# Attention, low-rank mixing and a two-layer MLP on one core: seven products instead of eight in one more part, with the input sums made earlier and the decoding placed by a table

## The chip, the cores and the metric

The kernel runs on one core of a Trainium2 chip. A core has five engines that each work through their own instructions in order and wait for one another by semaphores: TensorE (PE in the rows; PEld is its loading of weights, which overlaps the matmuls), VectorE (DVE), ScalarE (ACT), GpSimd (POOL) and SyncE (SP), whose queue issues the DMAs. The metric is the device time of one execution in microseconds (us), here the median of three runs.

## The reference

```python
# attention: 4 batches, 12 heads, 448 positions, head_dim 64
scores = scale * np.matmul(q, k.transpose(0, 1, 3, 2))
scores = np.where(causal_mask, -1000000000.0, scores)
attn = softmax(scores)
x = (attn @ v).transpose(0, 2, 1, 3).reshape(B, S, 768)
# low-rank mixing over positions: U (448 x 32), V (32 x 448)
h = x.transpose(0, 2, 1) @ U @ V
u = x + h.transpose(0, 2, 1)
# MLP: w_ch1 (768 x 3072), w_ch2 (3072 x 768)
ch = np.maximum(u @ w_ch1, 0.0) @ w_ch2
return u + ch
```

The weights arrive as 64-bit floats and are turned into 32-bit floats on the chip.

## The kernel before

**Stages.** Attention runs first, pair of heads by pair of heads. Then comes the MLP in two groups: `mlp()` for batches 0 and 1, `strassen()` for batches 2 and 3. The end of attention and of the mixing for the last batch (the *drain*) is woven into the first part of `mlp()`.

**The first group.** `mlp()` goes through the hidden units in six parts p = 0 to 5. A part has a first layer (four weight blocks n = 8p to 8p+3, 128x768 each) and a second layer (four more). Each number is split into a high and a low half, and a product is three matmuls (high-high, high-low, low-high). In a *plain* part the first layer takes both batches and both halves of the input rows by themselves: 4 blocks x 2 batches x 18 = 144 matmuls of 448 columns. In a part of `QUADS` (`range(3, FS - 1)`: p = 3 and 4) `quad()` uses Strassen's scheme with seven products instead of eight: two sets of 7 products x 9 = 126 matmuls. The second layer has 144 in both kinds. `quad()` needs sums of weight blocks (`sums13`, `sums24` in `quad_steps`, on VectorE, into `b_sums`), their split halves (`high` on ScalarE, `lows` on VectorE, for the four operands A1, S23, S1, A2 of a set) and sums of the inputs (tiles `T`, made once by `t_rounds`); its results pass through `r` and `r2`, where VectorE adds the products that share an output.

**Steps.** `mlp()` yields after each matmul, and nine of them are a *step* i, a tick of some 1.83 us. At each step the main loop emits what `schedule()` filed under it in `timed`, then the pending ReLUs, a share of the attention that is left (`DRAIN` = 32: it is spread over 32 steps), a round of `t_rounds`, a round of `u_rounds` (input sums for the second group) and, near the end, the first preparations for the second group. So the order on each engine is the order of emission.

**Decoding.** A block is loaded by `load_w` (SP queue), turned into bits by `w_bits` (two ScalarE and three VectorE instructions), added up by `w_sum` (GpSimd, tile `wa`, and a store to `kept` on the SP queue), and split by `w_high` (ScalarE) and `w_low` (VectorE, then a store to `halves`). `schedule()` gives `w_bits` fixed distances to the part's begin (`BITS`, or a pace of 13 or 16 steps in four blocks), and `w_sum` comes two steps later. `home(n)` names one of four places for `wa`.

**Input sums.** `t_rounds(kc)`, kc = 0 to 2, loads two kept pieces of the inputs from `plain_x`, makes two sums, splits them, makes two more and splits those: six rounds. Their tiles lie in the pools `b_top` and `b_late`, which open when the drain is over; a round is emitted every third step from then on (steps 37 to 88). The pool `b_early` opens when the last `values` of attention frees the heads' room.

## Time and profile before

| | before |
|---|---|
| median of 3 runs | 847.87 us (847.28 to 847.97) |
| the profiled execution | 846.55 us, its span 844.8 us |
| PE busy | 837.7 us (99%), 4708 instructions |
| PEld busy | 745.4 us (88%) |
| DVE busy | 690.9 us (82%) |
| ACT busy | 452.4 us (54%) |
| POOL busy | 234.5 us (28%) |
| DMA | 166.65 MB, mean 197 GB/s |

The busy time of an engine is a sum over stages that differ; the first group of the MLP lies between about 172 and 531 us of the span. A wait that the profile shows on one engine matters where TensorE waits in the end.

### The profile page before, as it was taken

Reading aid. Unit: us, or ns where it says so; the run is one execution under the profiler, and the core shown is the slowest. Engines: PE = TensorE matmul, PEld = TensorE weight load, DVE = VectorE, ACT = ScalarE, POOL = GpSimd, SP = SyncE. Lnnn points to the kernel's source line nnn. Section 1 sums busy time; section 2 is a strip of 40 time slices with the busy share of each in tenths; the row PEclk is TensorE's granted clock in tenths of the full one; section 3 lists DMA queues with packets and bytes.
Section 4 is the critical chain, followed back from the end, with each engine's and each line's share of the span. In section 5 each row is a group of like instructions: output and inputs, shape, how many; then the busy total and the mean of one; then the engine's idle time right before and its main releaser. Section 6 shows DMA issues by size and latency. Waiting matters only on the chain.

```text
span 844.8 us, 13959 instructions
## 1 busy us (share of the span) xinstructions
PE 837.7 (99%) x4708; PEld 745.4 (88%) x4708; DVE 690.9 (82%) x1436; ACT 452.4 (54%) x978; POOL 234.5 (28%) x305
## 2 busy tenths in 40 slices
PE   8999999999999999999999999999999999999998
PEld 6778777788999998998999999999999999999997
DVE  7988988965767888997988887698887887886795
ACT  7999999854325454546463553361533515335420
POOL 4765777732111223222312342010000001001100
PEclk9999999999999999999999999999999999999999
DMA  6554253475669777768764569944554544655334
GB/s 208 182 180 147 89 166 121 132 276 207 231 233 318 277 265 238 295 247 314 245 225 188 195 237 331 321 144 145 155 174 125 156 145 138 191 167 163 91 88 143
DMA packets 75816, 166.65 MB, mean 197 GB/s; under 512 B 7009, under 2 KB 49633, under 8 KB 75745
## 3 DMA queue, kind: packets, MB, share of 16 engines
q1 hardware_dynamic: 75744, 165.77, 58.3%
q8 instruction: 37, 0.61, 0.3%
q14 instruction: 35, 0.28, 0.1%
HBM read 104.79 MB, written 55.44 MB: 190 GB/s over the span
## 4 chain that ended last, share of the span: by engine, by line
PE 95%; DVE 3%; issue 1%; ACT 1%; POOL 0%; DVEq 0%; ACTq 0%; POOLq 0%
PE sa L1022 21%; PE of L726 21%; PE hf L666 13%; PE se L1022 10%; PE s L268 6%; PE t L322 5%; PE pv L338 5%; PE sb L1022 5%; PE ba L691 3%; PE y L396 1%; PE be L691 1%; PE bb L691 1%; DVE wsp L473 1%; PE xt L379 1%; DVE p L283 1%
## 5 line engine op out<-in xcount | busy, mean ns | idle before, releaser
L201 POOL TENSOR_TENSOR wa<-wld 128x768 int32<-128x768 int32 (+1 forms) x49 | 77.6, 1583 | 257.1 <-DVE wld L189 141.8
L726 PE MATMUL of<-g,wsp 128*128 128x448 f32 x630 | 132.7, 366 | 0.4 <-DVE wsp L473 0.3
L726 PEld LDWEIGHTS of<-g,wsp 128*128 128x128 f32 x630 | 117.9, 188 | 10.6 <-DVE wsp L473 1.5
L311 POOL TENSOR_SCALAR p<-p,r 112x112 f32<-112x112 f32 (+3 forms) x188 | 94.3, 522 | 56.9 <-DVE r L305 33.9
L818 POOL TENSOR_TENSOR wsp<-wld,wsp 128x256 fp32r<-128x256 f32 (+1 forms) x30 | 30.2, 1010 | 279.9 <-ACT wsp L968 159.5
L297 ACT ACTIVATE p<-p,m 112x112 f32<-112x112 f32 (+1 forms) x192 | 99.8, 527 | 8.6 <-DVE m L283 8.6
L1022 PE MATMUL sa<-h,wsp 128*128 128x448 f32 (+1 forms) x438 | 98.1, 364 | 0.0
L1022 PE MATMUL sa<-uch,wsp 128*128 128x448 f32 x288 | 88.8, 369 | 0.0
L1022 PEld LDWEIGHTS sa<-h,wsp 128*128 128x128 f32 x438 | 81.6, 188 | 6.9
L283 DVE CUSTOM_DVE_ANT_0 p<-s,mask 112x112 f32<-112x112 f32 x192 | 75.1, 445 | 12.4 <-PE s L268 9.5
L935 ACT CAST wsp<-sw 128x256 fp32r<-128x256 f32 (+3 forms) x60 | 34.1, 577 | 79.4 <-PE sa L1022 36.3
L666 PE MATMUL hf<-wsp 128*128 128x448 f32 x288 | 62.1, 368 | 0.0
L666 PE MATMUL hf<-u,wsp 128*128 128x448 f32 x288 | 61.4, 366 | 0.0
L484 ACT CAST wsp<-wa 128x768 fp32r<-128x768 f32 x34 | 28.3, 833 | 61.2 <-POOL wa L201 49.3
L1022 PEld LDWEIGHTS sa<-uch,wsp 128*128 128x128 f32 x288 | 54.1, 188 | 5.9 <-ACT r L1043 1.0
L818 DVE TENSOR_TENSOR xb<-sa,xb 128x448 f32<-128x448 f32 (+1 forms) x73 | 44.7, 615 | 17.1 <-PE sa L1022 16.8
L322 PE MATMUL t<-ident,p 112*112 112x112 f32 x480 | 56.7, 262 | 1.1 <-DVE p L311 0.7
L666 PEld LDWEIGHTS hf<-u,wsp 128*128 128x128 f32 x288 | 53.9, 188 | 4.3
L666 PEld LDWEIGHTS hf<-wsp 128*128 128x128 f32 x288 | 53.5, 188 | 4.3 <-DVE wsp L473 0.2
L737 DVE TENSOR_TENSOR xa<-of,xa 128x448 f32<-128x448 f32 x72 | 42.2, 617 | 18.4 <-PE of L726 18.4
L183 ACT ACTIVATE wa<-wld 128x768 f32<-128x768 f32 (+1 forms) x49 | 44.2, 902 | 23.3 <-DMA wld<-in_w_dram 11.7
L268 PE MATMUL s<-qk 64*112 64x224 f32 (+3 forms) x384 | 53.8, 415 | 0.8 <-DMA qk<-in_qk_dram 0.8
(150 smaller groups left out, 1785.5 us busy)
## 6 DMA issues: line engine op xcount, KB each, us to landing
wld<-in_w_dram SPq DMA_DIRECT2D x48, 768.0 KB, 6.0
kept<-wa SPq DMA_DIRECT2D x48, 384.0 KB, 3.2
halves<-wsp SPq DMA_DIRECT2D x23, 768.0 KB, 4.4
wsp<-halves SPq DMA_DIRECT2D x36, 384.0 KB, 4.1
wsp<-halves SPq DMA_DIRECT2D x54, 256.0 KB, 3.2
qk<-in_qk_dram SPq DMA_DIRECT2D x23, 448.0 KB, 4.8
wld<-kept SPq DMA_DIRECT2D x24, 384.0 KB, 4.5
wld<-kept SPq DMA_DIRECT2D x72, 128.0 KB, 2.8
```

The costliest lines, as they stand in the source:

```text
L183: nc.scalar.activation(f(a), f(hi), AF.Abs)
L201: nc.gpsimd.tensor_tensor(a.bitcast(I32), t[:, :n, 1].bitcast(I32), t[:, :n, 0].bitcast(I32), op=ALU.add)
L268: nc.tensor.matmul(o, t[r, q0 : q0 + CP], t[r, S // 2 : S // 2 + n], start=True, stop=True, skip_group_check=True,)
L283: nc.vector.tensor_tensor_reduce(out=st["p", b, h][:, POFF[i] : POFF[i] + n], in0=st.pop(("o", b, h, i)), in1=mask[:, S - n :], scale=-(D* ...
L297: nc.scalar.activation(pi, pi, AF.Exp, bias=m[:, i : i + 1], scale=-1.0, accum_out=l[:, i : i + 1])
L311: e.tensor_scalar(pi, pi, r[:, i : i + 1], 1.0, op0=ALU.mult, op1=ALU.mult)
L322: nc.tensor.transpose(o[:, n : n + CP], src, ident[:CP, :CP])
L338: nc.tensor.matmul(o[j * D : (j + 1) * D, kt * CP : S], v[:, kt, j, :], pt[:, n0 : n0 + S - kt * CP], start=j not in begun, stop=not left[ ...
L666: nc.tensor.matmul(o, w[:, l, cs], m, start=(kc + i == 0), stop=(kc + i == NC + 1))
L726: nc.tensor.matmul(o[k, b], w[:, l, cs], g[:, v], start=(half + m + i == 0), stop=(half + m + i == 4), skip_group_check=True,)
L818: (nc.vector if e == "V" else nc.gpsimd).tensor_tensor(o, a, b, op=op)
L1022: nc.tensor.matmul(st[bank, q][:, part], a, b[:, part], start=(n in FIRST and ms[0] == 0 and k == 0), stop=(n in LAST and end and k == len ...
```

## The change

`QUADS` begins at 2 instead of 3, so part 2 takes seven products too. To have the input sums by then, `t_rounds` runs in steps 16 to 53 (`T_AT`), and its tiles lie in a pool `b_in` that opens with the heads' room. Its rounds for one kc now follow one another. The step of each `w_bits` stands in a table (`BIT_AT`, 48 numbers), the distance to `w_sum` in another (`GAPS`), and that of each round of `u_rounds` in a third (`U_AT`, steps 141 to 183; before: every second step from 143 to 177). `DRAIN` is 34. The moves of x to `xr` in the drain are issued from the ScalarE queue. The first group has 186 steps instead of 188. Instructions that only check the order at build time (`owner`, `summed`) put nothing on the chip.

```diff
-DRAIN = 32
+DRAIN = 34
...
+T_LOADS = (15, 18, 35)
+T_AT = (16, 22, 23, 24, 25, 26, 27, 31, 32, 35, 38, 39, 41, 43, 46, 49, 51, 53)
...
-QUADS = range(3, FS - 1)
+QUADS = range(2, FS - 1)
...
-        nc.sync.dma_start(out=f(t), in_=st["x", b, c])
+        e = nc.scalar if "draining" in st else nc.sync
+        e.dma_start(out=f(t), in_=st["x", b, c])
...
-        if p in QUADS or p + 1 == QUADS[0]:
+        if 12 <= n <= 8 * QUADS[-1] + 7:
             return (2, 3, 0, 1)[j % 4]
-        return (j + (p == 0)) % 2
+        return (j + (p < QUADS[0])) % 2
...
-                bits = [(n0 + j, c + y) for j, y in enumerate(BITS)]
...
-                pace = 13 if p + 1 == QUADS[0] else 16
-                bits = [(n0 + j, c + pace * j // 4 - 7) for j in range(8)]
...
-            for n, y in bits:
-                sums[n] = y + 2
+            for n in range(n0, n0 + 8):
+                y = BIT_AT[n]
+                sums[n] = y + GAPS[n]
                 if n > 1:
                     at(y, w_bits, n)
-                    at(y + 2, w_sum, n)
+                    at(sums[n], w_sum, n)
...
         def loads():
...
+            if kc < 2:
+                tags = (("T24h1", "T24l1"), ("T13h2", "T13l2"))[kc]
+                x.extend(st["b_in"].tile([P, 2, S], F32, tag=tag, name="x") for tag in tags)
+            else:
+                x.extend((st["r"][:, :2], st["r2"]))
+            for y, c in zip(x, (kc, kc + NC // 2)):
+                for b in range(2):
+                    nc.sync.dma_start(out=y[:, b], in_=plain_x[c][:, b * S : (b + 1) * S])
...
-        return loads, [sums13, high("13"), lows("13")], [sums24, high("24"), lows("24")]
+        return loads, [sums13, high("13"), lows("13"), sums24, high("24"), lows("24")]
...
                 if step == values and a == pairs[-1]:
                     heads.close()
-                    b_pool(b_early, "b_early")
+                    b_pool(b_in, "b_in", "left")
+                    for kc in range(NC // 2):
+                        load, more = t_rounds(kc)
+                        at(T_LOADS[kc], load)
+                        rounds += more
...
-            if rounds and i >= t_begin and i % 3 == 1:
+            if i in T_AT:
                 rounds.pop(0)()
...
-            if us and US(i):
+            if i in U_AT:
                 for step in us.pop(0):
                     step()
```

**PE, the first layer of part 2.** Before, these rows stand between the second layers of parts 1 and 2 (`hf`: plain results; `wsp`: split weights; `u`, `g`: inputs of the two layers).

```order
L726 MATMUL of<-g,wsp 128x448 x144
L666 MATMUL hf<-wsp 128x448 x18
L666 MATMUL hf<-u,wsp 128x448 x18
L666 MATMUL hf<-wsp 128x448 x18
L666 MATMUL hf<-u,wsp 128x448 x18
L666 MATMUL hf<-wsp 128x448 x18
L666 MATMUL hf<-u,wsp 128x448 x18
L666 MATMUL hf<-wsp 128x448 x18
L666 MATMUL hf<-u,wsp 128x448 x18
L726 MATMUL of<-g,wsp 128x448 x144
```

After, the same place begins so (`ba`, `bb`, `be`: the shared outputs of the seven products; `wh`: two further places for split weights).

```order
L746 MATMUL of<-g,wsp 128x448 x144
L711 MATMUL ba<-wsp,wh 128x448 x9
L711 MATMUL bb<-wsp,wh 128x448 x9
L711 MATMUL ba<-T,wh 128x448 x9
L711 MATMUL be<-T,wh 128x448 x9
L711 MATMUL ba<-T,wsp 128x448 x9
L711 MATMUL ba<-wsp,wh 128x448 x9
L711 MATMUL bb<-wsp,wh 128x448 x9
L711 MATMUL ba<-u,wsp 128x448 x9
L711 MATMUL be<-T,wsp 128x448 x9
L711 MATMUL ba<-T,wh 128x448 x9
L711 MATMUL be<-T,wh 128x448 x9
```

Eight groups of 18 have become fourteen groups of 9, the last two of which stand between pieces of the second layer.

**DVE, steps 15 to 21 of the drain.** Before: a decoding (three rows that end in L189) follows `y`, the low half of the mixing's intermediate, which TensorE waits for at its next `hm`.

```order
L654 SCALAR_TENSOR_TENSOR g<-hf,g 128x448
L419 TENSOR_TENSOR xb<-hm,xb 128x448
L473 TENSOR_TENSOR wsp<-wa,wsp 128x768
L409 TENSOR_TENSOR y<-y 64x256
L185 TENSOR_SCALAR wa<-wa 128x768
L187 TENSOR_SCALAR wa<-wa 128x768
L189 SCALAR_TENSOR_TENSOR wld<-wld,wa 128x768
L388 TENSOR_TENSOR xn_l<-xt,xn_h 112x4x128
L737 TENSOR_TENSOR xa<-of,xa 128x448
```

After:

```order
L674 SCALAR_TENSOR_TENSOR g<-hf,g 128x448
L190 TENSOR_SCALAR wa<-wa 128x768
L192 TENSOR_SCALAR wa<-wa 128x768
L194 SCALAR_TENSOR_TENSOR wld<-wld,wa 128x768
L479 TENSOR_TENSOR wsp<-wa,wsp 128x768
L425 TENSOR_TENSOR xb<-hm,xb 128x448
L840 TENSOR_TENSOR x<-x 128x448 x2
L415 TENSOR_TENSOR y<-y 64x256
L757 TENSOR_TENSOR xa<-of,xa 128x448
L479 TENSOR_TENSOR wsp<-wa,wsp 128x768
```

The first two input sums (L840) now stand ahead of `y`, one step behind the issue of their loads on the SP queue:

```order
L490 DMA kept_102<-wa 128x768
L804 DMA x<-plain_x 128x448 x4
L472 DMA halves_150<-wsp 128x1536
L490 DMA kept_103<-wa 128x768
L804 DMA x<-plain_x 128x448 x4
L178 DMA wld<-in_w_dram 128x1536
```

The loads stand behind the store of the fifth block's sum; before, none stood in the drain.

**DVE, steps 26 to 31.** Before: the decodings of blocks 8 and 9 are one each, with only the outputs' sums (`xa`, `xb`) and one low half between them.

```order
L185 TENSOR_SCALAR wa<-wa 128x768
L187 TENSOR_SCALAR wa<-wa 128x768
L189 SCALAR_TENSOR_TENSOR wld<-wld,wa 128x768
L419 TENSOR_TENSOR xb<-hm,xb 128x448 x2
L737 TENSOR_TENSOR xa<-of,xa 128x448
L419 TENSOR_TENSOR xb<-hm,xb 128x448
L737 TENSOR_TENSOR xa<-of,xa 128x448 x2
L473 TENSOR_TENSOR wsp<-wa,wsp 128x768
```

After:

```order
L479 TENSOR_TENSOR T<-x,T 128x896
L425 TENSOR_TENSOR xb<-hm,xb 128x448
L840 TENSOR_TENSOR x<-x 128x448 x2
L757 TENSOR_TENSOR xa<-of,xa 128x448
L190 TENSOR_SCALAR wa<-wa 128x768
L192 TENSOR_SCALAR wa<-wa 128x768
L194 SCALAR_TENSOR_TENSOR wld<-wld,wa 128x768
L425 TENSOR_TENSOR xb<-hm,xb 128x448
L757 TENSOR_TENSOR xa<-of,xa 128x448 x2
L479 TENSOR_TENSOR wsp<-wa,wsp 128x768
L190 TENSOR_SCALAR wa<-wa 128x768
L192 TENSOR_SCALAR wa<-wa 128x768
```

An input sum's low half (`T`) and two further input sums have come in, and a second decoding follows the first at once.

## Rows read from the trace of the kernel before

**Rows 1.** The page: busy us of each engine, and the granted TensorE clock by slices.

```profile
PE 837.7 (99%) x4708; PEld 745.4 (88%) x4708; DVE 690.9 (82%) x1436; ACT 452.4 (54%) x978; POOL 234.5 (28%) x305
PEclk9999999999999999999999999999999999999999
```

**Rows 2.** Timeline of PE where parts 1 to 5 begin (start us, us).

```profile
244.62 0.57 PE L666 MATMUL hf<-wsp 128*128 128x448 f32 x2
...
302.99 0.97 PE L666 MATMUL hf<-wsp 128*128 128x448 f32 x4
...
362.02 1.99 PE L691 MATMUL ba<-wsp,wh 128*128 128x448 f32 x9
...
417.44 1.98 PE L691 MATMUL ba<-wsp 128*128 128x448 f32 x9
...
472.50 0.97 PE L666 MATMUL hf<-wsp 128*128 128x448 f32 x4
```

**Rows 3.** Waits of PE and of PEld, 160 to 535 us: total, times, longest.

```profile
PE of L726 <- DVE wsp L473: 0.3, 1, 0.3
...
PEld of L726 <- DVE wsp L473: 1.5, 3, 0.7
```

**Rows 4.** Busy us of PE, PEld, DVE, ACT, POOL, clock, DMA: parts 2, 3.

```profile
302.99:362.00 59.01, 58.70 (x289) 53.98 (x288) 53.55 (x74) 29.48 (x40) 17.01 (x10) 1.00 0.76 271
362.00:417.20 55.20, 55.05 (x270) 50.41 (x270) 48.92 (x75) 30.42 (x46) 12.49 (x8) 1.00 0.76 273
```

**Rows 5.** DVE groups of part 3, 362 to 417 us: count, busy us, mean ns.

```profile
L473 DVE TENSOR_TENSOR wsp<-sums,wsp 128x384 fp32r<-128x384 f32 x4 | 4.3, 1077 | 0.0
...
L818 DVE TENSOR_TENSOR sums<-wa 128x384 f32<-128x384 f32 x4 | 2.0, 546 | 0.0
L473 DVE TENSOR_TENSOR wh<-sums,wh 128x768 fp32r<-128x768 f32 x2 | 1.9, 974 | 0.0
L818 DVE TENSOR_TENSOR r<-bb,r 128x448 f32<-128x448 f32 x2 | 1.2, 622 | 1.5 <-ACT wa L183 1.5
```

**Rows 6.** Timeline of the SP queue and of DVE around step 16.

```profile
210.50 0.32 SPq L480 DMA_DIRECT2D kept<-wa  x1
...
212.78 0.47 SPq L370 DMA_DIRECT2D xr<-xb  x1
...
211.38 0.96 DVE L473 TENSOR_TENSOR wsp<-wa,wsp 128x768 fp32r<-128x768 f32 x1 [0.33 <-ACT wsp L484]
...
219.91 0.63 DVE L737 TENSOR_TENSOR xa<-of,xa 128x448 f32<-128x448 f32 x1 [4.09 <-PE of L726]
```

**Rows 7.** DMA issues of the page: KB of one, median us to landing.

```profile
xr<-xa SPq DMA_DIRECT2D x12, 224.0 KB, 2.3
...
r<-plain_x SPq DMA_DIRECT2D x3, 224.0 KB, 5.5
...
sums<-plain_x SPq DMA_DIRECT2D x1, 224.0 KB, 6.8
```

**Rows 8.** Busy us of each engine, steps 20 to 34 (columns as in rows 4).

```profile
219.91:249.05 29.14, 29.14 (x150) 26.99 (x149) 20.97 (x35) 7.89 (x12) 4.40 (x3) 1.00 0.52 183
```

**Rows 9.** DVE groups of part 2, 303 to 362 us: decodings, input sums' low halves.

```profile
L189 DVE SCALAR_TENSOR_TENSOR wld<-wld,wa 128x768 uint32<-128x768 uint32 x10 | 9.6, 960 | 0.4
...
L187 DVE TENSOR_SCALAR wa<-wa 128x768 uint32<-128x768 uint32 x10 | 5.6, 560 | 0.3
...
L473 DVE TENSOR_TENSOR T<-x,T 128x896 fp32r<-128x896 f32 x3 | 3.2, 1083 | 0.0
```

**Rows 10.** Timeline at two input sums, with the GpSimd addition beside the second.

```profile
325.57 0.62 DVE L818 TENSOR_TENSOR x<-x 128x448 f32<-128x448 f32 x1
...
325.87 1.64 POOL L201 TENSOR_TENSOR wa<-wld 128x768 int32<-128x768 int32 x1 [5.20 <-ACT g L650]
326.22 1.77 DVE L818 TENSOR_TENSOR x<-r,x 128x448 f32<-128x448 f32 x1
```

**Rows 11.** Timeline of DVE at step 3 of the drain.

```profile
183.28 0.63 DVE L654 SCALAR_TENSOR_TENSOR g<-hf,g 128x448 fp32r<-128x448 f32 x1 [3.63 <-ACT g L650]
```

**Rows 12.** DVE groups of the first group, 165 to 535 us: second group's input sums.

```profile
L818 DVE TENSOR_TENSOR ucl<-tmp,uch 128x896 fp32r<-128x896 f32 x6 | 8.7, 1450 | 0.0
```

More of the change, by code (lines that the diff above doesn't have):

```diff
@@ L473, in low @@
         (nc.vector if BE[key] == "V" else nc.gpsimd).tensor_tensor(o, a, b, op=ALU.subtract)
+    summed, owner = set(), {}
     def w_bits(n):
+        assert owner.get(home(n)) is None
+        owner[home(n)] = n
         st["wa", n] = decode_bits(st["wr", n], WB, home(n))
@@ L480, in w_sum, with used_up @@
         nc.sync.dma_start(out=kept[n], in_=f(st["wa", n]))
+        summed.add(n)
+    def used_up(n):
+        owner[home(n)] = None
+        return st.pop(("wa", n))
     def w_high(n, i):
+        assert n in summed
         t = st["w", n] = slot(i)
@@ L487, in w_low @@
         t = st["w", n]
-        low(key, t[:, 1], f(st.pop(("wa", n))), f(t[:, 0]))
+        low(key, t[:, 1], f(used_up(n)), f(t[:, 0]))
         keep_split(n, t)
@@ L543, in sums13 @@
         def sums13():
+            assert top in summed and bottom in summed
             s = st["b_sums"]
@@ L551, in sums24 @@
             adder(s[:, 3], a(1), s[:, 0], ALU.subtract)
+            owner[home(top)] = None
         def high(name, i, *parts):
             def step():
+                assert top in summed
                 if name not in g:
@@ L640, in activated @@
             return st["u1", 0][:, 0]
[L641 to L642 removed]
+        if n == 3 and b == 1:
+            pool, tag = (st["b_late"], "g13") if p else (st["b_in"], "T24l2")
+        else:
+            pool, tag = main, f"g{b}{n}"
+        return pool.tile([P, 2, S], F32R, tag=tag, name="g")
     def mlp():
@@ L770, in t_rounds @@
     def t_rounds(kc):
-        if kc:
-            x = st["b_late"].tile([P, 2 * WB], F32, tag=f"slot{kc + 1}", name="x")
-            x = x[:, : 3 * S].rearrange("p (i s) -> p i s", i=3)
-        else:
-            x = st["r"]
-        last = st["b_sums"].rearrange("p i c -> p (i c)")[:, :S] if kc == 2 else st["r2"][:, kc]
+        x = []
         parts = {}
         def loads():
-            low, high = plain_x[kc], plain_x[kc + NC // 2]
-            nc.sync.dma_start(out=x[:, 0:2].rearrange("p i s -> p (i s)"), in_=low)
-            nc.sync.dma_start(out=x[:, 2], in_=high[:, S:])
-            nc.sync.dma_start(out=last, in_=high[:, :S])
+            if kc < 2:
+                tags = (("T24h1", "T24l1"), ("T13h2", "T13l2"))[kc]
+                x.extend(st["b_in"].tile([P, 2, S], F32, tag=tag, name="x") for tag in tags)
+            else:
+                x.extend((st["r"][:, :2], st["r2"]))
+            for y, c in zip(x, (kc, kc + NC // 2)):
+                for b in range(2):
+                    nc.sync.dma_start(out=y[:, b], in_=plain_x[c][:, b * S : (b + 1) * S])
         def sums13():
-            adder(x[:, 0], x[:, 1], x[:, 0], ALU.subtract)
-            adder(x[:, 1], x[:, 2], x[:, 1], ALU.subtract)
+            a, b, _, c = (y[:, i] for y in x for i in range(2))
+            adder(a, b, a, ALU.subtract)
+            adder(b, c, b, ALU.subtract)
         def sums24():
-            adder(x[:, 0], x[:, 2], x[:, 0], ALU.subtract)
-            adder(x[:, 1], last, x[:, 0], ALU.subtract)
+            a, b, d, c = (y[:, i] for y in x for i in range(2))
+            adder(a, c, a, ALU.subtract)
+            adder(b, d, a, ALU.subtract)
         def high(key):
@@ L796, in step @@
                 parts[key] = [
-                    st["b_top"].tile([P, 2, S], F32R, tag=f"T{key}{l}{kc}", name="T") for l in "hl"
+                    st["b_in"].tile([P, 2, S], F32R, tag=f"T{key}{l}{kc}", name="T") for l in "hl"
                 ]
-                nc.scalar.copy(parts[key][0], x[:, :2])
+                nc.scalar.copy(parts[key][0], x[0])
             return step
@@ L805, in step @@
                 h, l = parts[key]
-                low(f"T{key}", l, x[:, :2], f(h))
+                low(f"T{key}", l, x[0], f(h))
                 if key == "24":
@@ L1322, in attention_mix_mlp @@
                     st["r2"] = st["b_top"].tile([P, 2, S], F32, tag="r2", name="r2")
-                    for kc in range(NC // 2):
-                        load, t13, t24 = t_rounds(kc)
-                        at(i + 1 + 4 * kc, load)
-                        rounds[3 * kc : 3 * kc] = t13
-                        rounds += t24
-                    t_begin = i + 6
             if i < NC:
                 keep_x(i)
-            if rounds and i >= t_begin and i % 3 == 1:
+            if i in T_AT:
                 rounds.pop(0)()
@@ L1355, in attention_mix_mlp @@
             emit(prep)
-        assert not us and not timed and not later
+        assert not us and not rounds and not timed and not later
         psx.close()
```

27 lines of the change are left out of this document (14 added, 13 removed).

## The prediction

> **What bounds the kernel now.** I read the page first, then the waits of TensorE, then the timeline of TensorE part by part, and only then the other engines in the stretches where the change puts work. The page says that PE is busy 99% of the span and that its clock is granted in full in every slice [rows 1]. That alone proves little, since matmuls overlap in the record. The waits settle it: between 160 and 535 us, which holds the whole first group, PE waits for another engine once, for 0.3 us, and the loading of weights waits for that same kind of low half three times, 1.5 us in all [rows 3]. So here a matmul is worth its spacing, and every other engine is worth nothing until it is late for TensorE.
>
> The starts of the parts give that spacing [rows 2]. Part 1 is plain, 288 matmuls, and takes 302.99 - 244.62 = 58.37 us, or 0.2027 us each. Part 2, plain too, takes 59.03 us (362.02 - 302.99). Parts 3 and 4 have seven products, 270 matmuls, and take 55.42 and 55.06 us; 270 x 0.2027 is 54.73, so they lose 0.3 to 0.7 us. The reader is to see that the trace already holds what part 2 is to become.
>
> **The change part by part.**
>
> *Part 2 with seven products.* Eighteen matmuls go (144 to 126; the order shows them gone): 18 x 0.2027 = 3.65 us. By whole parts it is 59.03 less the mean of parts 3 and 4 (55.24) = 3.79 us; the ends of that comparison are 58.37 - 55.42 = 2.95 and 59.03 - 55.06 = 3.97 us. I take 3.7, between the count and the mean, since both tell of the same matmuls.
>
> *What the seven products add on VectorE.* Per part: eight sums of weights at 0.55 us, two low halves of S23 at 0.97, two of S1 at 0.55 to 1.08 and six additions of products at 0.62 [rows 5]: 4.4 + 1.9 + 1.1 to 2.2 + 3.7, some 11 to 12 us. Part 2 has room for that only because the input sums leave it. The measure is part 3, which does exactly this work with the eight decodings that the table also puts into part 2: VectorE is busy 48.92 of 55.20 us there, and PE is busy 55.05 [rows 4]. Part 2 before is at 53.55 of 59.01, with ten decodings [rows 9] and more than half of the input sums. So the cover is 6 us wide, as in part 3, and the cost of this work on the path is what part 3 already loses, which the comparison by parts contains.
>
> *The input sums in the drain.* They move from steps 37 to 88 to steps 16 to 53. Two places matter. First, step 16: VectorE meets the first two sums one step behind the issue of their loads. The loads stand behind a store that was issued at 210.50 us; an issue takes up to 0.47 us [rows 6], so the fourth goes at about 210.9 + 3 x 0.47 = 212.3. A landing of this size takes 2.3 to 6.8 us, 5.5 for three loads from the same place [rows 7], so they are there at 214.6 to 219.1; I take 217.8. VectorE comes to the sums at about 214 (the low half at 211.38 [rows 6], a decoding that now stands ahead of it, 0.96 and twice 0.56 us [rows 9], and one addition), so it stands for 1 to 5 us. Queued behind it are `y`, for which TensorE's next `hm` waits, and the outputs' sums. Before, VectorE stood idle there for 4.09 us until PE released it at 219.91 [rows 6]. Two sums and `y` after 217.8 end at 219.5, and that `hm` comes one step later than before, near 220: cost 0, at most 0.8 us when the loads take 6.8.
>
> Second, steps 20 to 34. VectorE is busy 20.97 of 29.14 us there [rows 8], 8.17 free. There come in four input sums at 0.62 [rows 10] and three low halves at 1.08 [rows 9], 5.7 us, and the decoding of block 10, 2.1 us; two additions of the mixing at 0.62 go out to later steps, since the drain is spread over 34. Net 6.6 us in 8.17: it fits with 1.6 us to spare, and a low half of weights is emitted three steps, 5.5 us, ahead of its use. Cost 0, with the rival below for what it is if the room is gone.
>
> *The second group's sums.* The last low half now comes at step 183 of 186. It takes 1.45 us [rows 12] and its first reader is the third product of the second group, behind 18 matmuls (3.6 us) and the two steps that are left of the first group, also 3.6 us. Cost 0.
>
> *The rest.* Two decodings at step 0 put 2.1 us on VectorE ahead of what it did there, where it stands idle for 3.63 us three steps later [rows 11]: 0. The moves to `xr` take 0.47 us each [rows 6] from ScalarE instead of the SP queue, an engine at 54% [rows 1]: 0. The shorter distances to `w_sum` change when GpSimd may start, not how long it works: 0, and the same for the places of `wa`. If the cover of these is gone, each costs its own length, below 2.1 us; I keep 0.8 us for all of them in the range.
>
> [...] Rows 10 show what a neighbour costs VectorE: an input sum takes 0.62 us alone and 1.77 while GpSimd adds up a block, 1.15 more. [...]
>
> **The rivals.**
>
> *VectorE falls behind in the drain (slower).* Place: steps 20 to 34. Seven new instructions with two SBUF inputs can each meet a GpSimd addition, at 1.15 us [rows 10]. All seven make 8.1 us on top of the net 6.6, in 8.17 us of room: 6.5 us late. A mixing product whose bank waits for an addition emitted one step before has no lead, so PE would stand for up to these 6.5 us: 844.2 + 6.5 = 850.7. It makes the kernel slower by over 0.2% (1.7 us) from a wait of 5.4 us on, so nearly all seven must collide. GpSimd is busy 4.40 of 29.14 us there [rows 8], 15%, so one collision is to be expected, and that fits into the 1.6 us. Chance 0.09.
>
> *Part 2 doesn't have its operands in time (no change).* In parts 3 and 4 the operands are prepared under a part of the same kind; in part 2 the first set's sums and halves are made under part 1, beside the last input sums, and the decoding is tighter. Each of the eight operands could then make the weight load wait as the three in rows 3 did, 0.3 to 0.7 us: 2.4 to 5.6 us, which eats two thirds of the 3.7 or more. Time 846.6 to 849.8, by the near end 846.6 to 848. Against it: part 3 does it in 55.42 us with PE idle for 0.15 us [rows 4]. Chance 0.13.
>
> *The first loads hold the drain.* The case of step 16 at its bad end, with the landings of 6.8 us and what follows late: 0.8 to 1.5 us, 845.0 to 845.7. It is still faster. Chance 0.10, and 0.02 of it beyond, in no change.
>
> That the change doesn't do what it says is out: the order has the eighteen matmuls gone.
>
> **How the numbers follow.** The profiled execution took 846.55 us around a span of 844.8 us; less 3.7 that makes a span of 841.1 and 842.85 us. The median of the runs shown is 1.32 us above that execution, so I subtract from the median: 847.87 - 3.7 = 844.2 us. The forecast has 0.68, the loads 0.10, no change through late operands 0.13, slower through the drain 0.09. The low end is the largest saving (3.97) and the 0.59 us by which the fastest run lies below the median: 843.3. The high end takes in the forecast's 0.8, the loads and the nearer half of the second rival: 847.4. What lies beyond is some 0.16 above and 0.03 below. By a measurement that can tell 0.2% (1.7 us): faster 0.76 (forecast and nearly all of the loads), within 0.15, slower 0.09.
>
> **What would show it.** In the profile after, part 2's first matmul to part 3's should be 55 to 55.5 us instead of 59.03, with PE's waits between 160 and 535 us still under 1 us. VectorE should show one idle stretch of 1 to 5 us before the first input sum, put down to the load, and be busy some 27 of 29 us in steps 20 to 34. Wrong would be: a wait of PE for `y`, for `xb` or `xa` in the drain (first or third rival), or several waits of the weight load in part 2 for low halves or sums (second). If part 2 takes 55 us and the time is still above 846, the loss lies where I priced 0.

## The result, and the profile after

The changed kernel takes **840.59 us** (median; 839.75 to 841.97) where the kernel before takes 847.92 us beside it (847.28 to 848.54): a ratio of 0.9915, 95% interval 0.9898 to 0.9932. That is 7.3 us less. The forecast was 844.2 us, 3.7 less, and its range began at 843.3: the direction is right, and the gain is twice what was worked out and lies outside the range. The profiled execution took 839.75 us around a span of 838.0 us, 6.8 us less than the 844.8 us of before.

The page of after; the line answers to [rows 1]:

```profile
PE 831.4 (99%) x4690; PEld 742.0 (89%) x4690; DVE 697.0 (83%) x1456; ACT 457.3 (55%) x990; POOL 234.0 (28%) x305
PEclk9999999999999999999999999999999999999999
```

Eighteen matmuls are gone, VectorE works 6 us more, and the granted clock is 1.000 in the mean of the span, with a 9 in every slice, as before. So the gain is in matmuls and their spacing. The timeline of PE in the kernel after, where parts 0 to 5 begin (start us, us), answers to [rows 2]:

```profile
171.91 1.26 PE L686 MATMUL hf<-wsp 128*128 128x448 f32 x5
...
243.94 1.98 PE L686 MATMUL hf<-wsp 128*128 128x448 f32 x9
...
302.79 2.02 PE L711 MATMUL ba<-wsp,wh 128*128 128x448 f32 x9
...
358.10 1.99 PE L711 MATMUL ba<-wsp 128*128 128x448 f32 x9
...
412.66 2.02 PE L711 MATMUL ba<-wsp,wh 128*128 128x448 f32 x9
...
467.84 2.39 PE L686 MATMUL hf<-wsp 128*128 128x448 f32 x11
```

Part 2 now takes 358.10 - 302.79 = 55.31 us instead of 59.03: 3.72 us less, and 3.7 was forecast. The rest of the gain stands elsewhere. Part 3 takes 54.56 us instead of 55.42 [rows 2], though it has 270 matmuls in both. The second group, which the lines shown ahead of the prediction touch only by the steps of its input sums, is shorter too. Timeline of PE at its beginning and end, the kernel before:

```profile
531.10 0.37 PE L1022 MATMUL sa<-uch,wsp 128*128 128x448 f32 x1
...
534.79 0.37 PE L1022 MATMUL sa<-uch,wsp 128*128 128x448 f32 x1
...
839.71 1.49 PE L1022 MATMUL sa<-h,wsp 128*128 128x224 f32 x12
```

and the kernel after:

```profile
526.20 0.37 PE L1044 MATMUL sa<-uch,wsp 128*128 128x448 f32 x1
...
529.86 0.36 PE L1044 MATMUL sa<-uch,wsp 128*128 128x448 f32 x1
...
832.93 1.49 PE L1044 MATMUL sa<-h,wsp 128*128 128x224 f32 x12
```

From the first matmul to the last twelve it was 839.71 - 531.10 = 308.61 us and is 306.73 us. No wait has gone there; the matmuls themselves stand closer. Between the first and the second row shown lie 18 of them: 3.69 us before (some 205 ns each), 3.66 us after (some 203 ns).

The waits of the weight load between 160 and 535 us after (total, times, longest) answer to [rows 3]; PE itself has no wait left in the first group:

```profile
PEld of L746 <- DVE wsp L479: 0.4, 1, 0.4
```

Before, the weight load waited three times, 1.5 us in all, for low halves of the second layers' weights in `wsp` [rows 3], and a fourth time for one in `wh`, which rows 3 leave out:

```profile
PEld of L726 <- DVE wh L473: 0.4, 1, 0.4
```

These four have become one of 0.4, and PE's own 0.3 us is gone.

All differences by part, worked out as above from the first matmul of one part to that of the next (us; the second group to the start of its last twelve matmuls; the last column is the sum, the *MLP*). The recorded expectations count the second group to its last matmul, which adds 1.2 us. The table holds the kernels of the experiments too; their run medians come from several sets of runs, and the ratios below compare each with the kernel before in its own set:

| kernel | run median | part 0 | 1 | 2 | 3 | 4 | 5 | second group | MLP |
|---|---|---|---|---|---|---|---|---|---|
| before | 847.92 | 72.77 | 58.37 | 59.03 | 55.41 | 55.06 | 58.60 | 308.61 | 667.9 |
| after | 840.59 | 72.02 | 58.85 | 55.32 | 54.55 | 55.18 | 58.36 | 306.73 | 661.0 |
| after again (r1) | 840.83 | 72.00 | 58.86 | 55.32 | 54.55 | 55.18 | 58.36 | 306.73 | 661.0 |
| 96 bytes ahead of the left pools (r2) | 842.67 | 72.00 | 59.35 | 55.39 | 54.55 | 55.18 | 58.36 | 308.22 | 663.0 |
| 32 bytes (r8) | 843.11 (one run) | 72.02 | 59.35 | 55.33 | 54.55 | 55.18 | 58.36 | 308.12 | 662.9 |
| 64 bytes (r7) | 840.20 (one run) | 72.02 | 59.35 | 55.33 | 54.55 | 55.18 | 58.36 | 305.39 | 660.2 |
| all at multiples of 128 (r3) | 839.06 | 72.02 | 58.76 | 55.05 | 54.72 | 54.72 | 58.36 | 305.70 | 659.3 |
| the same again (r12) | 838.82 | 72.00 | 58.77 | 55.06 | 54.72 | 54.72 | 58.36 | 305.72 | 659.3 |
| the moved ones 64 behind (r11) | 838.73 | 72.00 | 58.77 | 55.04 | 54.68 | 54.66 | 58.37 | 305.33 | 658.9 |
| before, all at multiples of 128 (r5) | 846.54 | 72.69 | 58.37 | 59.23 | 55.41 | 55.06 | 59.17 | 306.40 | 666.3 |
| part 2 plain, old ticks (r4) | 846.82 | 72.35 | 58.85 | 58.44 | 55.32 | 55.47 | 59.69 | 306.84 | 667.0 |
| part 2 plain, table kept (r9) | 844.34 | 72.02 | 58.85 | 58.44 | 54.93 | 54.81 | 60.00 | 306.83 | 665.9 |
| seven products, old ticks (r6) | 847.24 | 72.74 | 62.98 | 55.39 | 54.97 | 55.58 | 58.36 | 306.72 | 666.7 |
| seven products, table to block 23 (r10) | 841.71 | 72.02 | 59.35 | 55.32 | 55.01 | 55.64 | 58.36 | 306.72 | 662.4 |

Two executions of the same kernel (after and r1, or r3 and r12) agree to 0.02 us in every part; what differs between them lies ahead, in attention. The granted clock is 1.00 between 175 and 830 us in every one of these profiles, and 0.98 to 1.00 ahead of 172 us (0.996 to 1.000 in the mean of the span). So the MLP column can be compared more finely than the run medians, which carry one or two microseconds (the single runs of after lie between 839.75 and 841.97 us).

A matmul of 448 columns is called *late* below where it starts 215 ns or more behind the one ahead of it; what it has over 202.7 ns is its lateness.

### The profile page after: what moved, and what is told of

Read it like the earlier page. It is cut to its first block, busy times and chain, and to the rows that moved or that the text cites. A ratio compares the mean times of both kernels' runs of the same rounds, so it can differ in the third digit from the quotient of the medians.

```text
span 838.0 us, 13967 instructions
## 1 busy us (share of the span) xinstructions
PE 831.4 (99%) x4690; PEld 742.0 (89%) x4690; DVE 697.0 (83%) x1456; ACT 457.3 (55%) x990; POOL 234.0 (28%) x305
## 4 chain that ended last, share of the span: by engine, by line
PE 97%; DVE 2%; ACT 0%; POOL 0%; issue 0%; DVEq 0%; POOLq 0%
PE sa L1044 21%; PE of L746 21%; PE hf L686 11%; PE se L1044 10%; PE s L273 6%; PE t L327 5%; PE pv L343 5%; PE sb L1044 5%; PE ba L711 5%; PE be L711 3%; PE y L402 1%; PE bb L711 1%; PE xt L385 1%; DVE p L288 1%; PE hm L420 1%; PE hm L421 1%
## 5 line engine op out<-in xcount | busy, mean ns | idle before, releaser
L746 PE MATMUL of<-g,wsp 128*128 128x448 f32 x594 | 125.3, 366 | 0.0
L746 PEld LDWEIGHTS of<-g,wsp 128*128 128x128 f32 x594 | 111.2, 188 | 9.3 <-DVE wsp L479 0.4
L840 POOL TENSOR_TENSOR wsp<-wld,wsp 128x256 fp32r<-128x256 f32 (+1 forms) x30 | 30.4, 1016 | 276.1 <-ACT wsp L990 156.5
L840 DVE TENSOR_TENSOR xb<-sa,xb 128x448 f32<-128x448 f32 (+1 forms) x73 | 44.6, 613 | 16.3 <-PE sa L1044 15.6
L327 PEld LDWEIGHTS t<-ident,p 112*112 112x112 f32 x480 | 47.7, 133 | 7.1 <-DVE p L316 0.7
L1044 PE MATMUL sa<-ucl,wsp 128*128 128x448 f32 x144 | 52.8, 366 | 0.0
L746 PE MATMUL of<-g,wh 128*128 128x448 f32 x252 | 52.4, 366 | 0.0
L746 PEld LDWEIGHTS of<-g,wh 128*128 128x128 f32 x252 | 47.3, 188 | 4.2
L1044 PE MATMUL se<-h,wsp 128*128 128x448 f32 x216 | 50.7, 365 | 0.0
```

Source lines behind the costliest of these rows:

```text
L327: nc.tensor.transpose(o[:, n : n + CP], src, ident[:CP, :CP])
L746: nc.tensor.matmul(o[k, b], w[:, l, cs], g[:, v], start=(half + m + i == 0), stop=(half + m + i == 4), skip_group_check=True,)
L840: (nc.vector if e == "V" else nc.gpsimd).tensor_tensor(o, a, b, op=op)
L1044: nc.tensor.matmul(st[bank, q][:, part], a, b[:, part], start=(n in FIRST and ms[0] == 0 and k == 0), stop=(n in LAST and end and k == len ...
```

## The experiments

**Two theories for the missing 3 us.** *Places*: the pools of the second group's inputs (tiles `uch`, `ucl`, three pairs) have moved in SBUF with `b_in`. In the built kernels all three pairs of before start 96 bytes behind a multiple of 128; after, two of them start at a multiple of 128 and one 96 behind. *Ticks*: the table of decodings takes away waits that the old rule had in all parts, and so gains in places that the prediction put at nothing. The rival to both is that the input sums or the seven products gave more than their count.

**r1: the changed kernel once more**, beside the other runs of that set.

> The changed kernel once more, beside the kernel before on the same chip. The parts of its first profile: part 2 took 55.32 us instead of 59.03, part 3 54.55 instead of 55.41, the second group 307.95 instead of 309.83. If the second group's gain of 1.9 us is the kernel's own, it comes again within 0.3 us; if it was that one execution (a rival: the chip was a little quicker that time), it does not, and the ratio moves from 0.9915 towards 0.9957, the 18 matmuls alone.

Measured 840.83 us, ratio 0.991 (0.9894 to 0.9926). The second group takes 306.73 us again, so its gain is the kernel's own and not the luck of one execution.

**r2: the pairs moved to 96.** The lines of the change that place them are these:

```diff
-                        tc.tile_pool(name=f"p_uc{kc}", bufs=1, side="right", reuse_waits="tile")
+                        tc.tile_pool(name=f"p_uc{kc}", bufs=1, side="right" if kc == 2 else "left", reuse_waits="tile")
```

In r2 an unused tile of 96 bytes stands ahead of the left pools:

```diff
                     b_in.close()
+                    ctx.enter_context(tc.tile_pool(name="pad", bufs=1, side="left", reuse_waits="tile")).tile([P, 24], F32, tag="pad", name="pad")
```

> The changed kernel with 96 bytes left free ahead of the second group's inputs in SBUF, so that all three pairs of them start 96 bytes behind a multiple of 128, as all do in the kernel before; in the changed kernel two of the three start at a multiple of 128. Nothing else moves. Theory of places (a moving operand that starts off a multiple of 128 costs some 2.5 ns a matmul): the mean spacing in the second group goes from 203.4 back to some 204.6 ns, 1.5 to 1.9 us over its 1517 matmuls, all of it in the second group. Rival (the second group gained from the ticks of its input sums, or by chance): no difference over 0.3 us there.

Measured 842.67 us, ratio 0.9932 (0.9915 to 0.9949): 1.8 us slower than r1. The unused tile is all that differs, and no instruction moves. (The last hidden values `h` of the second group come to lie in the same two pools, and move with them.) Timeline of PE in r2, the second group's ends:

```profile
528.89 0.37 PE L1044 MATMUL sa<-uch,wsp 128*128 128x448 f32 x1
...
837.11 1.49 PE L1044 MATMUL sa<-h,wsp 128*128 128x224 f32 x12
```

308.22 us against 306.73: 1.49 us come back in the second group. That is the size of *places* in the second group. Another 0.5 us comes in part 1, and it is not explained by starts, since no tile that part 1's matmuls read has moved. Timeline of PE there, first r2, then the kernel after:

```profile
264.76 3.88 PE L686 MATMUL hf<-u,wsp 128*128 128x448 f32 x18
268.48 3.88 PE L686 MATMUL hf<-wsp 128*128 128x448 f32 x18
```

```profile
262.57 3.81 PE L686 MATMUL hf<-u,wsp 128*128 128x448 f32 x18
266.22 3.81 PE L686 MATMUL hf<-wsp 128*128 128x448 f32 x18
```

Eighteen matmuls take 268.48 - 264.76 = 3.72 us (206.7 ns each) in one and 3.65 us (202.8 ns) in the other, with the same tiles at the same places. A stretch like this, 22 to 27 us long, is there in part 1 of r2, r7, r8 and r10 at the same place, in r6 some 5 us earlier, and not in the others. Each of these five was profiled once, so no run tells whether it belongs to the kernel or to the one execution. What makes it stays open.

**r7 and r8: which starts.** The same tile with 64 and with 32 bytes (`[P, 16]`, `[P, 8]`).

> As the run with 96 bytes ahead of the second group's inputs, but with 64: two of the three pairs start 64 bytes behind a multiple of 128. If what counts is a multiple of 64, the spacing of their matmuls stays at 202.8 ns; if it is 128, it goes to 205.

> The same with 32 bytes. If what counts is a multiple of 32, the spacing stays at 202.8 ns; if it is 64 or 128, it goes to 205 or above.

One run each: 840.20 and 843.11 us. In the second group 64 bytes cost nothing (305.39 us, 1.34 us less than after), and 32 bytes cost what 96 do (308.12 us). So the slow starts among these four are those that are no multiple of 64. But 64 is not the same as 128 either: the spacing did not stay at 202.8 ns, as the theory of 64 had it, but is 202.2 ns in the group's first 40 us (its first 18 matmuls take 3.64 us) and then rises to 206.7 ns for a while; r11 shows more of this.

**r3 and r12: everything at multiples of 128.** What is left at 96 in the kernel after stands at the right end of SBUF: the third pair, the places `wh` of split weights, and one `g`. The same unused tile of 96 bytes goes ahead of the right pools:

```diff
+                    ctx.enter_context(tc.tile_pool(name="pad", bufs=1, side="right", reuse_waits="tile")).tile([P, 24], F32, tag="pad", name="pad")
                     b_pool(b_late, "b_late", "right")
```

> The changed kernel with 96 bytes left free at the other end of SBUF when attention's room is given up, so that the third pair of inputs of the second group and the two further places for split weights (wh) start at multiples of 128 too. Theory of places: the second group gains 0.5 to 0.8 us more (252 matmuls with those inputs at 2.5 ns, and the last hidden ones), and parts 2 to 4, whose spacing was 203.6, 202.1 and 204.4 ns with wh off, come to 202.7 each: together 0.8 to 1.1 us less than the changed kernel. Rival: no difference.

> The changed kernel with 96 bytes put ahead of the right pools, so that every tile that moves through TensorE in the MLP starts at a multiple of 128: a second look at the version that measured 839.06 us. Theory 'the start of a tile in SBUF sets the spacing': 838 to 840 us, 1.0 to 2.5 us below the changed kernel, every stretch of the MLP at 202.7 ns. Rival 'the first measurement was luck': 840.3 us or more.

Measured 839.06 us, ratio 0.990 (0.9867 to 0.9932), and 838.82 us, ratio 0.9893 (0.9877 to 0.9908): 1.8 us quicker than r1 beside it in the first case. The second has no r1 beside it, and its MLP is that of the first to 0.02 us in every part. The second group's ends in r3:

```profile
525.06 0.37 PE L1044 MATMUL sa<-uch,wsp 128*128 128x448 f32 x1
...
528.71 0.36 PE L1044 MATMUL sa<-uch,wsp 128*128 128x448 f32 x1
...
830.76 1.50 PE L1044 MATMUL sa<-h,wsp 128*128 128x224 f32 x12
```

18 matmuls take 3.65 us, 202.8 ns each, and the group 305.70 us. From 240 us on, the mean spacing, late matmuls left out, is 202.6 to 202.8 ns in all but three of the ten-microsecond stretches of the MLP, and at most 203.4 in those. Part 4 goes from 55.18 to 54.72 us, which is 270 x 0.2027: there `wh` and the one `g` at 96 were the whole loss. But part 3, with the same places, goes the other way, from 54.55 to 54.72. Weights that start at 96 are both slower and quicker than those at a multiple of 128. Timeline of PE in part 2 of the kernel after, two groups of nine with weights in `wh` and then two more:

```profile
306.50 2.02 PE L711 MATMUL ba<-T,wh 128*128 128x448 f32 x9
308.37 2.01 PE L711 MATMUL be<-T,wh 128*128 128x448 f32 x9
...
319.40 1.97 PE L711 MATMUL ba<-T,wh 128*128 128x448 f32 x9
321.20 1.96 PE L711 MATMUL be<-T,wh 128*128 128x448 f32 x9
```

The first nine take 1.87 us, the third nine 1.80 us, with the same kind of operands. All groups of nine with weights in `wh` in parts 2 to 4 run at 205.4 to 206.7 ns or at 199.7 to 200.6 ns; in r3 they run at 202.2 to 203.0 ns. Which of the two comes when, no run tells.

**r5: the same 96 bytes in the kernel before**, ahead of its right pools.

```diff
+                    ctx.enter_context(tc.tile_pool(name="pad", bufs=1, side="right", reuse_waits="tile")).tile([P, 24], F32, tag="pad", name="pad")
```

> The kernel before with nothing changed but 96 bytes left free at the end of SBUF from which the second group's inputs are given their room, so that all three pairs start at a multiple of 128. Theory of places: the second group goes from 309.83 to some 307.5 us (751 matmuls with these inputs and 120 with the last hidden ones at 2.5 ns make 2.2 us), the first group stays: 845.6 us. Rival (the gain there came with the ticks): no difference.

Measured 846.54 us, ratio 0.9985 (0.9968 to 1.0001), with 848.23 us for before. The interval takes in 1, so the run times show no difference for sure; in the MLP it is 1.5 us, with the second group 2.2 us shorter and parts 2 and 5 longer by 0.2 and 0.6 us. Parts 2 and 5, and the second group up to 570 us, hold stretches at 206.7 ns like that of r2, so the gain is partly hidden. Behind those 570 us the second group runs at 202.7 ns, where before has up to 205.4, and 206.7 from 573 to 595 us.

**r11: the same tiles 64 behind.** 64 bytes ahead of the left pools and 32 ahead of the right ones, so that all three pairs, `wh` and the last `g` start 64 behind a multiple of 128.

```diff
+                    ctx.enter_context(tc.tile_pool(name="pad", bufs=1, side="right", reuse_waits="tile")).tile([P, 8], F32, tag="pad", name="pad")
                     b_pool(b_late, "b_late", "right")
...
                     b_in.close()
+                    ctx.enter_context(tc.tile_pool(name="padl", bufs=1, side="left", reuse_waits="tile")).tile([P, 16], F32, tag="padl", name="padl")
```

> The changed kernel with 64 bytes put ahead of the left pools and 32 ahead of the right ones, so that all three pairs of the second group's inputs, the places wh and the last g start 64 bytes behind a multiple of 128. Theory 'a start at any multiple of 64 is alike': as with all of them at a multiple of 128, 839.1 us within 1 us, the second group's matmuls 202.7 ns apart. Rival 'moving tile and weights 64 apart are quicker still' (with two pairs at 64 stretches of the second group ran at 200 to 202.1 ns): second group 2 to 4 us shorter than 306.9 us, time 835.5 to 837.5 us.

Measured 838.73 us, ratio 0.9889 (0.9873 to 0.9905), the same as r12. The first theory holds for the time, and the rival of 2 to 4 us falls, but the way there is not what either said. Timeline of PE in r11, first `uch` and `ucl`, then `h`:

```profile
527.00 0.37 PE L1044 MATMUL sa<-uch,wsp 128*128 128x448 f32 x1
...
528.81 0.36 PE L1044 MATMUL sb<-uch,wsp 128*128 128x448 f32 x1
...
622.04 2.64 PE L1044 MATMUL sa<-h,wsp 128*128 128x448 f32 x12
624.52 1.40 PE L1044 MATMUL se<-h,wsp 128*128 128x448 f32 x6
```

The nine matmuls of the inputs take 1.81 us (201 ns; 200.0 over longer stretches), and twelve of `h` take 2.48 us, 206.7 ns each, though that `h` has not moved and ran at 202.7 in r3. The two cancel in the sum. So in these runs the start of the moving tile changes the spacing (3.69 us for 18 matmuls of the inputs in r2, 3.65 in r3), but it is not all that sets it, and no run here tells what else does.

**r6: the changed kernel with the old ticks.** The table is filled by the rule of before, and `w_sum` comes two steps later everywhere.

```diff
-BIT_AT = (0, 0, 0, 0, 8, 13, 15, 20, 25, 28, 29, 35, 38, 42, 46, 47, 50, 53, ...
+BIT_AT = (-7, -3, 1, 5, 9, 13, 17, 21, 25, 28, 31, 34, 38, 41, 44, 47, 51, 53, ...
-GAPS = (3, 1, 3, 2, 3, 2, 2, 1, 2, 3, 2, 2, 2, 3, 0, 3, 1, 2, 0, 1, 3, ...
+GAPS = (2,) * 48
```

> The changed kernel with the table of ticks undone: each block decoded where the rule of the kernel before would put it for seven products in parts 2 to 4, the sum two steps behind. If the table removed the late low halves of parts 3 to 5 (0.69, 0.32 and 0.23 us of late matmuls before, 0 after), they come back: 0.7 to 1.5 us more. If the early input sums removed them, the late matmuls stay under 0.5 us in all and the time within 0.5 us of the changed kernel.

Measured 847.24 us, ratio 0.9994 (0.9982 to 1.0006): **without the table the run times show no gain at all.** In the MLP 1.2 us is left, less than the 1.5 us of the places. Neither theory had this. The late low halves of parts 3 and 4 do come back, 0.40 and 0.35 us, and part 5 shows none; but the bulk is in part 1, which no expectation named: part 2 keeps its 55.39 us, and part 1 takes 62.98 us instead of 58.85. Of these 4.1 us 3.7 are late matmuls, and the rest is the stretch at 206.7 ns. Waits in part 1 of r6, 244 to 303 us:

```profile
PEld of L746 <- DVE wsp L479: 3.0, 1, 3.0
PE of L746 <- DVE wsp L479: 2.6, 1, 2.6
```

One low half of weights is late by 3 us (two others, of the first layer's weights, make the weight load wait 1.1 us). Why, the timelines of DVE and ACT in r6 tell (in brackets the idle time before, and what ended it):

```profile
268.70 0.62 DVE L840 TENSOR_TENSOR r<-r 128x448 f32<-128x448 f32 x1
269.36 1.77 DVE L840 TENSOR_TENSOR r<-r,r 128x448 f32<-128x448 f32 x1
...
273.72 0.56 DVE L190 TENSOR_SCALAR wa<-wa 128x768 f32<-128x768 f32 x1 [2.06 <-ACT wa L188]
...
276.33 2.05 DVE L479 TENSOR_TENSOR wsp<-wa,wsp 128x768 fp32r<-128x768 f32 x1
...
271.22 0.94 ACT L821 CAST T<-r 128x896 fp32r<-128x896 f32 x1 [2.62 <-DVE r L840]
272.06 0.83 ACT L500 CAST wsp<-wa 128x768 fp32r<-128x768 f32 x1
272.80 0.89 ACT L188 ACTIVATE wa<-wld 128x768 f32<-128x768 f32 x1
```

The input sums stand behind a decoding here. The second takes 1.77 us instead of 0.62, while GpSimd adds up a block beside it (269.02 to 270.64 us). ScalarE stands for 2.62 us with the split of that sum at the head of its queue; behind it wait the first step of a decoding and the high half of the next weights. VectorE, whose next instructions are the rest of that decoding, then stands for 2.06 us. The low half comes behind the decoding and meets the next addition of GpSimd (276.10 to 277.57 us): 2.05 us instead of 0.95. It ends at 278.4 us; PE has waited for it for 2.6 us. In the kernel after, the sums stand ahead of that decoding and meet no addition, the decoding behind them finds its input ready, and the low half ends before PE comes to the second layer at 273.5 us (DVE):

```profile
265.76 0.62 DVE L840 TENSOR_TENSOR r<-r,r 128x448 f32<-128x448 f32 x1
266.31 0.55 DVE L190 TENSOR_SCALAR wa<-wa 128x768 f32<-128x768 f32 x1
...
271.19 0.95 DVE L479 TENSOR_TENSOR wsp<-wa,wsp 128x768 fp32r<-128x768 f32 x1
```

This chain is read from one trace. How much of it is the order and how much the two additions, no run separates.

**r4: seven products and table undone, input sums early.** `QUADS` from 3, the old ticks (two later behind part 2's first layer), the old steps of `u_rounds`; `T_AT`, `b_in` and `DRAIN` as after.

```diff
-QUADS = range(2, FS - 1)
+QUADS = range(3, FS - 1)
```

> The changed kernel with eight products in part 2 and the decoding at the places of the kernel before (every block as there, the sum two steps behind), but with the input sums early and the pools as changed. By the count of matmuls it is 3.65 us slower than the changed kernel. If the early input sums took the late low halves of weights away, part 2 loses nothing (58.4 us instead of 59.03) and the parts 2 to 5 show under 0.5 us of late matmuls (1.9 before); if the table of ticks did, they show 1 to 2 us of them again. The second group keeps its 1.9 us by the theory of places. In all 843.8 to 845.5 us.

Measured 846.82 us, ratio 0.998 (0.9971 to 0.999), above the expected 843.8 to 845.5. Early sums alone bring little: part 2 drops from 59.03 to 58.44 us, since no low half is late there any more. In parts 3 and 4 low halves stay late, 0.77 us together, so the early sums did not remove those. At the end of part 5 a new wait comes in, so that r4 is some 1.3 us worse than a clean undoing would be (waits, 160 to 545 us):

```profile
PEld sa L1044 <- DVE xa L757: 1.3, 1, 1.3
```

**r9: the table without the seven products.** As r4, but with the table and the steps of `u_rounds` of after, two ticks later behind tick 78.

```diff
-BIT_AT = (0, 0, 0, 0, 8, 13, 15, ... 70, 75, 78, 81, 83, 88, 90, ...
+BIT_AT = (0, 0, 0, 0, 8, 13, 15, ... 70, 75, 78, 83, 85, 90, 92, ...
-QUADS = range(2, FS - 1)
+QUADS = range(3, FS - 1)
```

> The changed kernel with part 2 plain again (288 matmuls instead of 270) and the tables kept, each entry behind tick 78 moved two ticks later. Theory 'the table gives by itself': the late low halves of parts 3 to 5, 2.1 us of late matmuls in the same kernel without the table, are gone (below 0.5 us in all), and the time is 1.5 to 2.5 us below that kernel's 846.8 us: 844.3 to 845.3 us. Rival 'the table only pays where seven products crowd part 1': the time stays at 846.3 to 847.3 us. By the second, seven products and the table are one gain of some 6 us that neither gives alone.

Measured 844.34 us, ratio 0.9962 (0.9951 to 0.9974). The time is where the first theory put it, 2.5 us below r4. But r4 belongs to another set on another chip; by the two ratios the difference is 1.5 us, and the MLP says only 1.1 us (667.0 to 665.9): parts 0, 3 and 4 give 0.3, 0.4 and 0.7, and the wait at the end of part 5 takes 0.3 back (it is 1.8 us here). The rest of the 2.5 lies in attention, which the table doesn't touch, or in what separates two sets of runs. In parts 1 to 5, low halves of the weights are no longer late at all. The expectation's 2.1 us of late low halves was misread: 1.3 of it was the wait for `xa`, and 0.77 were low halves. So the table, here with the steps of `u_rounds`, gives something by itself, about half of what was expected.

**r10: the table up to block 23, the old rule behind.**

```diff
-BIT_AT = (..., 81, 83, 88, 90, 92, 97, 105, 108, 111, 113, 118, 119, 123, 127, 135, 137, ...
+BIT_AT = (..., 81, 83, 86, 89, 93, 100, 105, 108, 111, 113, 116, 119, 123, 130, 135, 138, ...
```

`GAPS` is 2 from block 24 on.

> The changed kernel with the table for blocks 0 to 23 (the decodings of parts 0 to 2's weights) and the old rule, with two steps to the sum, for blocks 24 to 47. Theory 'what the table saves is in part 1': part 1 takes 58.4 to 59.4 us instead of 62.98 under the old rule, parts 3 and 4 lose some 0.4 us each again, time 841.3 to 842.5 us. Rival 'the saving is spread over all parts': part 1 still loses 1 us or more and the time is 844 us or more.

Measured 841.71 us, ratio 0.9929 (0.9913 to 0.9946), as the first theory had it. Part 1 is back at 59.35 us (0.5 of it the stretch at 206.7 ns), and parts 3 and 4 lose 0.46 us each. Waits for low halves in `wsp`, 160 to 535 us (one for `wh`, 0.4 us, comes on top):

```profile
PEld of L746 <- DVE wsp L479: 0.9, 2, 0.4
```

## Why the prediction fell short

**Part 2's matmuls: right, to two hundredths by luck.** 3.7 us was forecast, 3.72 came. The 18 matmuls are 3.65 us, as counted. Beside them 0.67 us of late low halves of before's part 2 went (58.44 in r4 and r9, where none is late), and the seven products brought 0.36 us of late ones and some 0.2 us of wider spacing (55.05 us in r3). These three nearly cancel.

**VectorE in part 2: right.** The windows of the kernel after (columns as in rows 4), part 2, part 3, steps 20 to 34, and part 1:

```profile
302.79:358.10 55.31, 55.29 (x271) 50.51 (x270) 48.76 (x75) 30.36 (x46) 12.10 (x8) 1.00 0.78 281
358.10:412.66 54.56, 54.56 (x272) 50.73 (x270) 47.88 (x74) 29.02 (x44) 12.00 (x8) 1.00 0.75 264
219.24:248.38 29.14, 29.14 (x150) 26.98 (x149) 27.66 (x43) 12.08 (x17) 5.87 (x4) 1.00 0.60 215
243.94:302.79 58.85, 58.85 (x292) 54.50 (x291) 55.54 (x77) 30.62 (x42) 16.74 (x10) 1.00 0.81 289
```

VectorE is busy 48.76 of 55.31 us in part 2, as part 3 had it before (48.92 of 55.20) [rows 4].

**The first input sums: cost right, picture wrong.** Timeline of SPq and of DVE at step 16 of the kernel after; it answers to [rows 6]:

```profile
208.27 0.32 SPq L490 DMA_DIRECT2D kept<-wa  x1
208.68 1.89 SPq L804 DMA_DIRECT2D x<-plain_x  x4
...
213.69 0.62 DVE L425 TENSOR_TENSOR xb<-hm,xb 128x448 f32<-128x448 f32 x1
214.22 2.02 DVE L840 TENSOR_TENSOR x<-x 128x448 f32<-128x448 f32 x2
...
219.24 0.62 DVE L757 TENSOR_TENSOR xa<-of,xa 128x448 f32<-128x448 f32 x1 [2.54 <-PE of L746]
```

VectorE never stands for the loads: they were issued from 208.68 us on, some 2 us earlier than I had, because the store ahead of them went at 208.27 instead of 210.50. My 1 to 5 us of idle time did not come, and neither did the third rival's case. VectorE came to the sums at 214.22 us; the terms that I had added up for that (211.38, a decoding of 0.96 and twice 0.56, a low half of 0.96, an addition of 0.62) make 215.0, not my 214, which changes nothing here.

**Steps 20 to 34: right.** Busy 27.66 of 29.14 us; 27 was forecast. Of the seven new instructions one met an addition of GpSimd, as many as were expected, and took 2.15 us instead of 1.08:

```profile
233.17 1.47 POOL L206 TENSOR_TENSOR wa<-wld 128x768 int32<-128x768 int32 x1 [8.41 <-DVE wld L194]
233.44 2.15 DVE L479 TENSOR_TENSOR T<-x,T 128x896 fp32r<-128x896 f32 x1
```

The two sums of step 16 met another (2.02 us instead of 1.25). Nothing on TensorE waits for them in this stretch.

**The step that failed: "the rest", priced at 0, and a sum that held nothing but part 2.** "The rest" held the new distances of the decoding, with a bound on what they could cost (0.8 us) and none on what they could give; the sides of the second group's pools were not in the sum at all. In place of 0 the runs showed about 0.9 us for the one and 1.5 us for the other.

*Low halves that were late already.* I had read three waits and 1.5 us for them [rows 3], and 0.3 to 0.7 us a part, and carried that loss over as belonging to the kind of part. It belonged to the ticks: with the table, no matmul of parts 3 to 5 is late, and r10 brings back 0.46 us each in parts 3 and 4 by the old rule alone. The late matmuls of before make 0.69, 0.32 and 0.23 us in parts 3, 4 and 5: 1.2 us, all gone. For part 5's 0.23 us the table is not shown to be the reason, since they don't come back under the old rule in r6 and r10.

*The places of the second group's inputs.* 1.5 us, shown by r2. The pools of two of the three pairs go from the right side of SBUF to the left one, by the lines shown with r2. The prediction left out an edit that only names a side, and never asked at which byte the tiles come to lie. The remaining 0.4 us of the second group's 1.88 is not explained by these places: in the profile of before, a stretch of `h` from 573 to 595 us runs at 206.7 ns, as part 1 of r2 does, and the second group of r2 has none there. Timeline of PE, the kernel before:

```profile
579.94 2.64 PE L1022 MATMUL sa<-h,wsp 128*128 128x448 f32 x12
582.42 1.40 PE L1022 MATMUL sb<-h,wsp 128*128 128x448 f32 x6
```

Twelve matmuls take 2.48 us.

Together: 3.7 (part 2) + 1.2 (late low halves) + 1.5 (places) + 0.4 (that stretch) + 0.3 (parts 0 and 1 together) - 0.3 (`wh` and one `g` at 96: part 4 loses 0.46, part 3 gains 0.17) = 6.8 us, which is the difference of the two profiles' MLP. The 7.3 us of the run medians holds 0.5 more that the profiles don't show.

**The rivals.** VectorE falling behind was the right mechanism at the wrong place. I looked for it in steps 20 to 34; it sits in part 1, to which the change brings 10 us of VectorE's work (VectorE busy 45.29 of 58.37 us before, 55.54 of 58.85 after), and which my sum never looked at. It decides once the ticks are the old ones: 3.7 us of late matmuls in r6. In r6 a sum takes 1.77 us and a low half 2.05 us, which both begin beside a GpSimd addition and end after it; in the kernel after they take 0.62 and 0.95 us, where no addition stands beside them. Why they take longer, no run shows. The second rival, late operands in part 2, came only in small: all late matmuls of part 2 make up 0.36 us. Its premise was misread, though: part 3 of before also has its first operands made under a plain part, and lost 0.69 us to late matmuls. So the forecast's zero for part 1 was right only because of an edit that I had priced at nothing.

The seven products and the table are therefore one change. By the MLP column, with neither it is 667.0 us (r4, of which 1.3 us is a wait of its own); with seven products alone 666.7 (r6), nothing; with the table alone 665.9 (r9, of which such a wait is 1.8 us); with both 661.0 (r1).

## What to carry to other kernels

When TensorE is the bound, read its spacing for each tile, not only its waits: where matmuls of the same form differ by a per cent without any wait (205 and 202.8 ns here), look at where their operands lie, since an edit that opens or moves a pool moves those (1.49 us in the second group of r2). When work is moved, add up the busy time of the engine that takes it in every stage that it lands in; a stage that goes from 13 us of room to 3, as part 1 did, needs its order looked at, even if the sum fits (3.7 us of late matmuls in r6). A small wait in each of several stages need not be a property of the stages: ask which order of emission makes it, before carrying it over into the forecast.

## What the runs showed of the hardware

**In these kernels the start of an operand in SBUF changes the spacing of matmuls.** With 448 columns and 128x128 weights that start at multiples of 128 bytes, 18 matmuls of the second group's inputs take 3.65 us (202.8 ns each) where the moving tile starts at a multiple of 128 (r3), and 3.69 us (205 ns) where it starts 96 behind one (before and r2). An unused tile that moves two of the three pairs from the one to the other takes the second group from 306.73 us (after) to 308.22 (r2). Starts 32 behind are as slow there (308.12 us, one run), and starts 64 behind are as quick in the sum (305.33 us in r11, 305.70 in r3), by way of stretches at 200.0 and at 206.7 ns. Groups of nine with weights that start 96 behind, and the moving tile at a multiple of 128, run at 205.4 to 206.7 ns or at 199.7 to 200.6 (`wh` in the kernel after), and parts 3 and 4 at 202.7 in the mean once these weights and the one `g` start at a multiple of 128 (r3: 54.72 us for 270 matmuls in each).

**Three levels, not explained.** 200.0, 202.7 and 206.7 ns come back in these profiles with a granted clock of 1.00. Starts alone don't set them: stretches of 20 to 66 us at 206.7 ns occur with tiles that run at 202.7 ns in another kernel from the same places (18 matmuls of part 1 take 3.72 us in r2 and 3.65 in after; the same in r5, which has all of them at multiples of 128, and in part 1 of five kernels). No run here tells what does.

**In two kernels TensorE's part of the time repeats to 0.02 us.** These are the two that were profiled twice (after and r1, r3 and r12): every part of the MLP is the same to 0.02 us, so that a change of a few tenths of a microsecond can be read from one profile, as long as no stretch at 206.7 ns falls into one and not the other. Run medians need several runs for it: the single runs of after lie between 839.75 and 841.97 us.
